# Maxima taken 162 slots ahead, 22 bursts without them, and keys and queries loaded apart for maxima and scores

## The chip, the cores and the metric

The kernel runs on one core of a Trainium2 chip. The metric is device time in microseconds of one execution; before the change it is 1759.31 us, the median of three runs (1758.76 to 1759.72).

## The reference

Two attention layers with 32 heads of 16 over the same input x (2048 rows of 512) are mixed by a gate.

```python
g = _sigmoid((x * gate_w).sum(-1, keepdims=True))
a = _A_ref(x, A_wqkv, A_wo)          # full softmax attention, 2048 x 2048 for each head
b = _B_ref(x, B_wq, B_wk, B_wv, B_wo, B_beta)
return g * a + (1 - g) * b
```

A is ordinary attention: `softmax(q k^T / 4) v`, then an output product. B cuts the sequence into four segments of 512. Inside a segment it is causal softmax attention; to that comes, for the segments after the first, `phi(q) M / (phi(q) z)` from a running memory `M = sum phi(k) v^T`, `z = sum phi(k)` over the earlier segments, mixed by `sigmoid(beta)` for each head. All arithmetic is float32; the kernel writes a factor as a high and a low part in a rounded float32 form and multiplies (high, low), (low, high) and (high, high).

## The kernel before, in words

**Units, slots, bursts.** The work on scores is cut into units `(side, g, c)`: four heads (`g` of 8 groups) and a chunk `c` of 512 queries. An A unit has 64 slots (4 heads x 16 blocks of 128 keys), a B unit 10. They alternate, A0, B0, A1, B1 and so on, 32 of each, 2368 slots in all. In a slot TensorE makes one score product (`score_part`, line 1063: 128 keys x 512 queries into one of three banks `st`), and ScalarE takes its exponential (line 1086, or 1083 for two of B's slots) into a tile `p`. A burst is three slots; behind them TensorE multiplies earlier `p` by the values (`some_values`, line 155, bank `ops`), or makes other products.

**Maxima.** The softmax needs the maximum of each query's scores first. So every score is also made the other way round (`max_product`, line 242: 128 queries x 512 keys, into one of four banks `sm`), and VectorE reduces it (line 275 for A; for B's triangle a masked form, line 290). There are as many maxima parts as slots (list `maxs`). Part `m = n + LEAD` is made in slot `n`, with `LEAD = 96`; the first 96 are made before the first score. When a unit's parts are done, GpSimd joins them (`finish_max`), TensorE transposes them (`transpose_max`), and two small transfers put them, high and low part, into rows 48 and 49 of the unit's tile of queries. The same rows of the tiles of keys hold ones, so that the score product subtracts the maximum.

**Tiles.** A tile of queries or keys is 128 x 2 x 512: two heads in each half of the partitions, at rows 0 and 64. Of each half 48 rows are the high and low parts (queries high, high, low; keys high, low, high), and two are the maxima or ones. Scores and maxima read the same tile: the keys wait in a ring of 8 (A) or 2 (B) from their maxima to their scores, the queries in a ring of 6. A product uses only one half of TensorE's rows, so a score on one half and a maximum on the other stand beside each other: slot `n` has its score on half `n % 2`, its maximum on the other.

**DRAM.** The projections write queries and keys to DRAM as 32 rows (16 high, 16 low; `qd`, `kd`); a tile of A is loaded by four transfers (16 and 32 rows for each half), one of B by six. All run on SyncE's queue, in order. Loads run `PRE = 20` parts ahead of the maxima; the last value product of a burst waits for the loads that the next burst needs (`wait_early`).

**Before the first score** come the projections, in steps of 12 matmuls of 512 columns (`slot()`, line 366), with a hand-written table of what follows in which step. 38 steps are A's, 48 are B's (four chunks of four query, four value and four key tiles); `s0` is B's first. A tile goes from its bank through ScalarE (`full`, then its high part, lines 432 and 433), and VectorE subtracts for the low part (line 440). In 24 of B's steps, from the twelfth on, a group of four maxima follows the products (`some_max`).

**Beside the scores** in the main loop: the output product of the chunk before, and for the first eight A units a projection of later queries. Both are lists of 12 (`shared`), four in a burst, so three bursts behind each A unit's end carry them instead of values; each is two products of 64 rows, one into `ops`, one into an `sm` bank that is lent for the time (`row_halves`). At the end ScalarE copies both banks out and GpSimd adds them (`join_halves`, lines 972 and 973). In the last 90 slots (`wide`) there are no maxima left to make.

Of the kernel before, what the change touches and what calls it, by code (L numbers as in the profile page):

```python
# [21 lines left out]
DH = 16  # L22
CH = 512
# [20 lines left out]
NKA, NKB = 8, 2  # L44
# [3 lines left out]
def gated_mix(ctx, tc, x, xT, wqkv, a_wo, b_wq, b_wk, b_wv, b_wo, beta, gate_w, out):  # L48
# [48 lines left out]
    qp = ctx.enter_context(tc.tile_pool(name="qp", bufs=6))  # L97
# [16 lines left out]

    maxs = []
    for k in range(NU):
        mine = {u: iter(range(32)) for u in range(2)}
        bs = [k - 1] if 0 < k < NU - 1 else [k - 1, k] if k else []  # L120
        theirs = {r: [(unit("B", b), (r, i)) for b in bs for i in range(5)] for r in range(2)}
        start, apart = (33, (3, 3)) if k == 1 else (6, (9, 3)) if k < NU - 1 else (23, (3, 3))
# [13 lines left out]
    assert len(maxs) == nS and all(first[u] + LEAD - last_max[u] > 24 for u in units)  # L136

    qt, kt_ = {}, {}

    def raw(t):  # L140
# [16 lines left out]
    def wait_early(n):  # L157

        loads_ = []
        for m in range(n + 1 + LEAD, n + 1 + BURST + LEAD):  # L160
            if m < nS:
                u, (r, i) = maxs[m]
                loads_ += lands.pop(("q", u, r), []) + lands.pop(("k", u, r, u[2] if u[0] == "B" else i // 8), [])
        for u, j in slots[n + 1:n + 1 + BURST]:
# [6 lines left out]
    def load_rows(t, r, src, hs, side, halves):  # L171

        if side == "B":
            return [nc.sync.dma_start(raw(t)[64 * r + 16 * i:64 * r + 16 * i + 16], src[x, hs].rearrange("h d t -> d h t"))  # L174
                    for i, x in enumerate(halves)]
        at_ = (0, 16, 48) if halves[1] == 0 else (0, 32, 48)
        return [nc.sync.dma_start(raw(t)[64 * r + a:64 * r + b], src[0:b - a, hs]) for a, b in zip(at_, at_[1:])]

    def load_q(u):
        side, g, c = u  # L180
        t = qp.tile([128, 2, CH], F32R, tag="q", name=f"q{side}{g}{c}")
        src = qd[side, g // 2, c]
        for r in range(2):
            hs = slice(4 * (g % 2) + 2 * r, 4 * (g % 2) + 2 * r + 2)
            lands["q", u, r] = load_rows(t, r, src, hs, side, (0, 0, 1))
        qt[u] = t

    def load_k(u, kc):
# [1244 lines left out]
```

## Time and profile before

| | |
|---|---|
| median of three runs | 1759.31 us |
| the profiled execution, its own time | 1757.79 us |
| span of its profile, first to last instruction | 1756.1 us |
| first score on TensorE | 280.08 us |
| busy: TensorE matmul, VectorE, ScalarE, GpSimd | 1747.3, 1600.3, 1449.4, 774.3 us |
| granted TensorE clock | 1.00 throughout |

The profile is of one execution; its times stand from the span's start. Line numbers (L275) are those of the kernel. In rows, `out<-in` are tiles, "PE" is TensorE, "PEld" its weight loads, "DVE" VectorE, "ACT" ScalarE, "POOL" GpSimd, "SP" SyncE. The end of a matmul is modelled, so a full PE line does not say that TensorE is at its peak; for the other engines busy time is what they ran.

### The profile page before, as it was taken

The numbers are of one execution on the slowest core, as the hardware profiler recorded it, in microseconds if no ns is written. First come the engines' busy times: TensorE is split into PE (matmuls) and PEld (weight loads), VectorE is DVE, ScalarE is ACT, GpSimd is POOL, SyncE is SP. The second block draws the span as 40 slices with busy tenths as digits, with TensorE's granted clock in tenths as the row PEclk, the third lists the DMA queues.
The fourth block names the chain that finished last, engine by engine and source line by source line (L and its number), as shares of the span: only waits on it lengthen the run. The fifth ranks groups of instructions, "written<-read, shape, count | busy, mean of one in ns | idle before, by whom it ended". The sixth has DMA issues, their size and how long they took to land.

```text
span 1756.1 us, 43955 instructions
## 1 busy us (share of the span) xinstructions
PE 1747.3 (100%) x16365; PEld 951.2 (54%) x16365; DVE 1600.3 (91%) x3327; ACT 1449.4 (83%) x2793; POOL 774.3 (44%) x1022
## 2 busy tenths in 40 slices
PE   9999999999999999999999999999999999999999
PEld 7887775555454454455444445455545445545454
DVE  7757788999999999999999999999999999999931
ACT  6545557898898988888889888888898889888884
POOL 3543233334453437453535454545344353545452
PEclk9999999999999999999999999999999999999999
DMA  6786567435453435444545454444444443444542
GB/s 209 258 285 222 199 217 218 117 98 139 122 155 110 137 110 165 142 136 135 143 122 151 126 142 129 133 142 124 148 130 146 130 135 111 144 125 133 150 160 62
DMA packets 149396, 261.77 MB, mean 149 GB/s; under 512 B 39064, under 2 KB 61624, under 8 KB 148672
## 3 DMA queue, kind: packets, MB, share of 16 engines
q1 hardware_dynamic: 146640, 254.42, 48.1%
q0 software_dynamic: 2400, 4.29, 0.9%
q8 instruction: 130, 2.13, 0.5%
q14 instruction: 82, 0.67, 0.1%
q10 hardware_dynamic: 144, 0.26, 0.1%
HBM read 174.39 MB, written 83.25 MB: 147 GB/s over the span
## 4 chain that ended last, share of the span: by engine, by line
PE 97%; DMA 1%; POOL 1%; ACT 0%; SPq 0%; DVE 0%; issue 0%; ACTq 0%; DVEq 0%; POOLq 0%
PE ops L155 35%; PE st L1063 27%; PE sm L242 15%; PE pr L366 9%; PE sm L155 4%; PE pair L366 4%; PE mt_ps L232 0%; PE tps L831 0%; PE sm L1063 0%; POOL rcp L1187 0%; SPq L174 0%; DMA vs<-wqkv 0%; ACT p L1086 0%; DMA qA<-qdA 0%; PE mps L845 0%; DMA qB<-mt 0%
## 5 line engine op out<-in xcount | busy, mean ns | idle before, releaser
L1086 ACT ACTIVATE p<-st 128x512 f32<-128x512 f32 x2261 | 1188.4, 605 | 139.9 <-PE sm L242 91.3
L275 DVE TENSOR_REDUCE pm<-sm 128x1 f32<-128x512 f32 x2048 | 1276.1, 681 | 14.6 <-PE sm L242 11.9
L242 PE MATMUL sm<-kA,qA 48*128 48x512 f32 x2048 | 694.7, 433 | 0.1
L1063 PE MATMUL st<-qA,kA 50*128 50x512 f32 x2014 | 665.8, 433 | 0.0
L155 PE MATMUL ops<-p,vA 128*17 128x256 f32 (+3 forms) x7160 | 560.9, 414 | 2.6 <-DMA rec<-odB 2.1
L1063 PEld LDWEIGHTS st<-qA,kA 50*128 50x128 f32 x2014 | 331.2, 185 | 388.6 <-ACT p L1086 349.1
L242 PEld LDWEIGHTS sm<-kA,qA 48*128 48x128 f32 x2048 | 339.2, 185 | 23.7 <-DVE pm L275 8.4
L155 PEld LDWEIGHTS ops<-p,vA 128*17 128x17 f32 x7160 | 149.9, 96 | 227.2 <-issue 186.7
L1187 POOL TENSOR_TENSOR rcp<-rec,minus 128x32 f32<-128x32 f32 x43 | 234.8, 5460 | 59.8 <-DMA rec<-dend 55.4
L290 DVE CUSTOM_DVE_ANT_0 rest<-sm,mask 128x128 f32<-128x128 f32 (+3 forms) x512 | 246.2, 481 | 3.9 <-PE sm L242 3.5
L1067 POOL TENSOR_SCALAR_AFFINE_SELECT p<-p 128x512 f32<-128x512 f32 x128 | 79.5, 637 | 293.4 <-ACT p L1086 283.2
L242 PE MATMUL sm<-kB,qB 48*128 48x128 f32 (+3 forms) x512 | 160.1, 373 | 0.0
L1063 PE MATMUL st<-qB,kB 50*128 50x512 f32 (+1 forms) x495 | 98.6, 319 | 0.3 <-ACT mt L235 0.3
L1063 PEld LDWEIGHTS st<-qB,kB 50*128 50x128 f32 x495 | 72.2, 186 | 47.0 <-ACT p L1086 32.2
L214 POOL TENSOR_TENSOR dm<-pm 128x32 f32<-128x32 f32 x32 | 7.9, 246 | 185.3 <-DVE pm L275 185.3
L155 PE MATMUL ops<-p,vB 128*17 128x128 f32 (+3 forms) x1504 | 87.9, 350 | 0.0
L242 PEld LDWEIGHTS sm<-kB,qB 48*128 48x128 f32 x512 | 84.5, 184 | 0.7
L437 POOL TENSOR_SCALAR mn<-full 128x512 f32<-128x512 f32 x24 | 37.0, 1542 | 75.5 <-ACT full L432 75.5
L223 POOL CAST ms<-pm 128x16 fp32r<-128x16 f32 x32 | 6.3, 196 | 124.0 <-DVE pm L290 124.0
L155 PEld LDWEIGHTS ops<-p,vB 128*17 128x17 f32 x1504 | 33.4, 96 | 28.6 <-issue 27.4
L1203 POOL TENSOR_TENSOR v<-v,inv 128x512 f32<-128x512 f32 x31 | 39.8, 1284 | 20.1 <-DMA inv<-rdA 12.3
L155 PE MATMUL sm<-wA,blk 64*128 64x512 f32 (+1 forms) x144 | 46.7, 405 | 0.0
(325 smaller groups left out, 1905.4 us busy)
## 6 DMA issues: line engine op xcount, KB each, us to landing
kA<-kdA SPq DMA_DIRECT2D x256, 128.0 KB
vA<-vdA SPq DMA_DIRECT2D x31, 544.0 KB
kA<-kdA SPq DMA_DIRECT2D x256, 64.0 KB
qB<-qdB SPq DMA_DIRECT2D x192, 64.0 KB
kB<-kdB SPq DMA_DIRECT2D x192, 64.0 KB
kdA<-q SPq DMA_DIRECT2D x32, 256.0 KB
qdB<-q SPq DMA_DIRECT2D x32, 256.0 KB
qA<-qdA SPq DMA_DIRECT2D x64, 128.0 KB
```

The costliest lines, as they stand in the source:

```text
L155: behind[0] = nc.tensor.matmul(*args, **kw)
L214: nc.gpsimd.tensor_sub(dm, pm[:, :, :, 2:4], pm[:, :, :, 0:2])
L242: nc.tensor.matmul(ps[:, n0:n0 + n], rows(qt[u][:, :, s * 128:(s + 1) * 128], h, 48), rows(k[:, :, k0:k0 + n], h, 48), start=True, stop=True)
L275: nc.vector.tensor_reduce(pm[:, h, s, kc:kc + 1], ps, axis=AX.X, op=ALU.max, negate=True)
L290: nc.vector.tensor_tensor_reduce(out=tri["rest"][:, 0:w], in0=ps[:, n0:n0 + w], in1=tri["mask"][:, CH - w:], scale=-1.0, scalar=3.0e38, op ...
L366: nc.tensor.matmul(ps, l, r, start=start, stop=stop)
L437: nc.gpsimd.tensor_scalar_min(ph["mn"], full, 0.0)
L1063: nc.tensor.matmul(ps[:, n0:n0 + CH - q0], rows(k[:, :, b * 128:(b + 1) * 128], h, 50), rows(q[:, :, q0:], h, 50), start=True, stop=True)
L1067: nc.gpsimd.affine_select(out=x, in_=x, pattern=[[0, 4], [1, 128]], base=0, channel_multiplier=-1, compare_op=ALU.is_ge, fill=0.0)
L1086: nc.scalar.activation(p[:, h], ps, AF.Exp, scale=SCALE)
L1187: eng.tensor_tensor(r, rec, minus, op=ALU.pow)
L1203: eng.tensor_mul(k["v"], k["v"], k["inv"])
```

## The change

- `FIRST = LEAD + len(thin)`, 162 maxima parts, are made before the first score. `some_max` follows each of B's steps 4 to 47 but steps 18, 30 and 42. The first loads are issued at `s0`, `s0 + 1`, `s0 + 2`. B's first maxima now begin with the main loop.
- For each of the first 22 A units one burst is `thin`: it has no maxima. It is the burst behind the unit's last output products, the one in which the two banks are copied out. `due_at[n]` says which part is due in slot `n`; behind the 22nd thin burst the lead is 96 parts as before.
- `half` and `heads_of` choose the head of each slot so that a score stands on the other half than the maximum beside it, since the parity of maxima shifts by three at each thin burst.
- `qd`, `kd` have 48 rows, in the order of the tile, so that a tile is loaded by two transfers of 48 rows; each projection tile is stored by three transfers instead of two (its high part twice for keys and queries alike).
- Tiles are loaded once for maxima (rings of 3 for A keys, 2 for B keys, 2 and 2 for queries) and once more for scores (4 A keys, 1 B keys, 2 A queries, 1 B queries), the latter `AHEAD = 24` slots ahead (`score_loads`). The rows of maxima are sent to the score tile when it is loaded, or when they are transposed, whichever is later. Only the score rings need rows of ones.
- The low parts of B's projection tiles, and those of B's three weights, are subtracted on GpSimd instead of VectorE.
- The closing tiles have buffers of their own choice.

```diff
-NKA, NKB = 8, 2
+NK = 10
+AHEAD = 24
+THIN = 22
...
-                rows_ = [32, 8, CH] if side == "A" else [2, 8, DH, CH]
+                rows_ = [48, 8, CH]
...
+    thin = set()
+    for k in range(THIN):
+        t = -(-(end[unit("A", k)] + 2) // BURST) * BURST + 3 * BURST
+        thin.update(range(t, t + BURST))
+    FIRST = LEAD + len(thin)
+    due_at = [FIRST]
+    for n in range(nS + LEAD):
+        due_at.append(due_at[-1] + (n not in thin))
...
-        bs = [k - 1] if 0 < k < NU - 1 else [k - 1, k] if k else []
+        bs = {0: [], 1: [], 2: [0], 3: [1, 2], NU - 1: [k - 1, k]}.get(k, [k - 1])
...
-    kbuf = {"A": [kp.tile([128, 2, CH], F32R, name=f"kA{i}") for i in range(NKA)],
-            "B": [kp.tile([128, 2, CH], F32R, name=f"kB{i}") for i in range(NKB)]}
-    knext = {"A": 0, "B": 0}
+    kbuf = [kp.tile([128, 2, CH], F32R, name=f"k{i}") for i in range(NK)]
+    qbuf = [kp.tile([128, 2, CH], F32R, name=f"q{i}") for i in range(6)]
+    ring = {("k", "A", 1): kbuf[0:4], ("k", "B", 1): kbuf[4:5], ("k", "A", 0): kbuf[5:8], ("k", "B", 0): kbuf[8:10],
+            ("q", "A", 1): qbuf[0:2], ("q", "A", 0): qbuf[2:4], ("q", "B", 0): qbuf[4:6]}
...
-        for m in range(n + 1 + LEAD, n + 1 + BURST + LEAD):
+        for m in range(due_at[n + 1], due_at[n + 1 + BURST]):
...
+    def load_rows(t, src, g):
+
+        hs = 4 * (g % 2)
+        return [nc.sync.dma_start(raw(t)[64 * r:64 * r + 48], src[:, hs + 2 * r:hs + 2 * r + 2]) for r in range(2)]
...
+    def store_rows(dst, side, keys, low, t):
+
+        for i in ((1,) if low and keys else (2,) if low else (0, 2) if keys else (0, 1)):
+            to = dst[16 * i:16 * i + 16]
+            if side == "A":
+                nc.sync.dma_start(to.rearrange("d h t -> (d h) t"), t)
+            else:
+                nc.sync.dma_start(to.rearrange("d h t -> h d t"), t)
...
+    def score_loads(n):
+
+        if n < nS:
+            u, j = slots[n]
+            if j == 0:
+                load_q(u, 1)
+            if j % 16 == 0:
+                load_k(u, u[2] if u[0] == "B" else j // 16, 1)
...
-                nc.vector.tensor_sub(q2, full, q1.bitcast(F32))
+                (nc.gpsimd if side == "B" else nc.vector).tensor_sub(q2, full, q1.bitcast(F32))
...
-        staged(tiles_w("k", "wk"), b_wk, ((raw_tile, 33, 2), (raw_tile, 35, 0)), [(41 + k, 3) for k in range(KT)], nc.gpsimd)
+        staged(tiles_w("k", "wk"), b_wk, ((raw_tile, 33, 2), (raw_tile, 35, 0)), [(41 + k, 3) for k in range(KT)], nc.gpsimd, eng=P)
...
-        for i, t in enumerate(kbuf["A"] + kbuf["B"]):
+        for i, t in enumerate(kbuf[0:5]):
...
-        for n in range(5):
-            post_at(s0 + 6 + 3 * n, 2, lambda n=n: loads(16 * n))
+        for n in range(3):
+            post_at(s0 + n, 2, lambda n=n: loads(16 * n))
+        for n in range(AHEAD):
+            post_at(s0 + 36 + n // 3, 1, lambda n=n: score_loads(n))
-        for n in range(12, 64):
+        for n in range(4, 48):
             if n in (18, 30, 42):
                 post_at(s0 + n, 3, lambda c=n // 12: mem_q(c))
-            elif n // 12 > 2 or n % 12 < 8:
+            else:
                 post_at(s0 + n, 3, some_max)
...
-        h = (0, 2, 1, 3)[j % 4]
+        h = heads_of[n]
...
+        score_loads(n + AHEAD)
         if n < nS:
             score_part(n)
-        m = n + LEAD
-        if m < nS:
+        m = due_at[n] if n < nS + LEAD else n + LEAD
+        if n not in thin and m < nS:
             loads(m + PRE)
```

More of the change, by code (lines that the diff above doesn't have):

```diff
@@ L113, in gated_mix @@
     nS = len(slots)
+    thin = set()
[6 more added lines that the diff above has]
+        due_at.append(due_at[-1] + (n not in thin))
+    slot_of = {due_at[n]: n for n in range(nS) if n not in thin}
+    n_of = lambda m: slot_of.get(m, m - FIRST)
     maxs = []
@@ L348, in gated_mix @@
             nc.tensor.matmul(idle[:, :128], identf, identf, start=True, stop=True)
-        ones = wk1.tile([2, CH], F32, name="ones")
-        nc.vector.memset(ones, 1.0)
+        one = wk1.tile([128, CH], F32, tag="mn", name="one")
+        nc.vector.memset(one[0:2], 1.0)
+        ones = dr.tile([2, CH], F32, name="ones")
+        nc.gpsimd.dma_start(ones, one[0:2])
         now = [0]
@@ L416, in xchunk, with qk_tile @@
             return xT[:, c * CH:(c + 1) * CH]
-        def qk_tile(w, xc, o, dst, then=None, side="B", bank=None):
+        def qk_tile(w, xc, o, dst, then=None, side="B", bank=None, keys=False):
             ps = bank() if bank else pr_ps.tile([128, CH], F32, tag="pr", name="pr")
@@ L705, in tiles_x2 @@
         def tiles_x2():
-            x2["t"] = [[qp.tile([128, 2, CH], F32R, tag="q", name="x2") for _ in range(2)] for _ in range(2)]
+            x2["t"] = [qbuf[2:4], qbuf[4:6]]
             xs[2] = lambda a, k: x2["t"][a][k // 2][:, k % 2]
@@ L907, in gated_mix @@
             slot()
-        assert not rows_left
+        assert not rows_left and mnext[0] == FIRST
     gp = ctx.enter_context(tc.tile_pool(name="gp", bufs=1, reuse_waits="tile"))
@@ L1046, in gated_mix @@
     queue = []
+    heads_of = {}
+    for u in units:
+        for j0 in range(0, SLOTS[u[0]] - 3, 4):
+            of = {0: [0, 1], 1: [2, 3]}
+            for j in range(j0, j0 + 4):
+                heads_of[first[u] + j] = of[half[first[u] + j]].pop(0)
+        if u[0] == "B":
+            for j in (8, 9):
+                heads_of[first[u] + j] = 2 * half[first[u] + j]
     def score_part(n):
```

136 lines of the change are left out of this document (76 added, 60 removed).

## The prediction

> **What bounds the kernel now.** I read the page first, then the windows (busy time of each engine per stretch), then the time line of single engines inside two stretches: the one in which maxima are left out, and the one that takes them over.
>
> ```profile
> span 1756.1 us, 43955 instructions
> PE 1747.3 (100%) x16365; PEld 951.2 (54%) x16365; DVE 1600.3 (91%) x3327; ACT 1449.4 (83%) x2793; POOL 774.3 (44%) x1022
> ...
> DVE  7757788999999999999999999999999999999931
> ```
>
> TensorE is busy all the time, but its matmul ends are modelled, so this only says that it never waits long. VectorE's line of digits changes at slice 7: before it, in the projections, VectorE has room; behind it, in the main loop, it has none. The windows (columns: PE, PEld, DVE, ACT and POOL busy with their instruction counts, clock, DMA share, GB/s) say it in numbers:
>
> ```profile
> 100.00:125.00 25.00, 25.00 (x112) 20.70 (x111) 16.65 (x25) 13.48 (x24) 13.85 (x21) 1.00 0.94 320
> 121.16:142.93 21.77, 21.77 (x98) 17.98 (x96) 7.73 (x14) 12.12 (x21) 8.39 (x12) 1.00 0.85 288
> 177.03:188.05 11.02, 11.02 (x50) 9.07 (x49) 9.17 (x18) 5.93 (x11) 4.59 (x3) 1.00 0.84 318
> 400.00:500.00 100.00, 100.00 (x1036) 49.44 (x1030) 99.67 (x214) 89.67 (x175) 46.48 (x65) 1.00 0.48 136
> 327.31:331.46 4.15, 4.15 (x40) 1.87 (x36) 4.15 (x12) 4.15 (x9) 3.14 (x4) 1.00 0.00 0
> 740.26:744.39 4.13, 4.13 (x40) 1.86 (x36) 4.13 (x12) 4.13 (x9) 3.21 (x4) 1.00 0.52 142
> 1012.71:1016.85 4.14, 4.14 (x40) 1.86 (x36) 4.14 (x12) 4.14 (x9) 3.21 (x4) 1.00 0.61 153
> ```
>
> The first three lie in the projections, the fourth in the middle of the main loop: VectorE 99.67 of 100 us, ScalarE 89.67. The last three are, for A units 0, 9 and 15, the two bursts behind the unit's last output products (a burst is three score slots and what TensorE does behind them). There ScalarE too is busy without a gap, 4.13 of 4.13 us. That is where the change acts, so I look inside, at A unit 9, whose scores end at slot 730 and whose thin burst is slots 741 to 743. ScalarE, VectorE and TensorE there:
>
> ```profile
> 739.12 1.09 ACT L1083 ACTIVATE p<-st 128x512 f32<-128x512 f32 x2 [0.49 <-PE st L1063]
> 740.09 0.61 ACT L1086 ACTIVATE p<-st 128x512 f32<-128x512 f32 x1
> 740.56 0.61 ACT L972 COPY res<-ops 128x512 f32<-128x512 f32 x1
> 741.03 0.63 ACT L973 COPY bot<-sm 128x512 f32<-128x512 f32 x1
> 741.50 3.11 ACT L1086 ACTIVATE p<-st 128x512 f32<-128x512 f32 x6
> 744.93 0.60 ACT L1086 ACTIVATE p<-st 128x512 f32<-128x512 f32 x1 [0.32 <-PE sm L242]
> 742.27 2.52 DVE L275 TENSOR_REDUCE pm<-sm 128x1 f32<-128x512 f32 x4
> 744.97 1.29 DVE L275 TENSOR_REDUCE pm<-sm 128x1 f32<-128x512 f32 x2 [0.17 <-PE sm L242]
> 740.26 0.45 PE L242 MATMUL sm<-kB,qB 48*128 48x128 f32 x2
> 741.56 0.84 PE L155 MATMUL ops<-p,vB 128*17 128x384 f32 x8
> 742.33 0.50 PE L1063 MATMUL st<-qA,kA 50*128 50x512 f32 x1
> 743.20 0.49 PE L1063 MATMUL st<-qA,kA 50*128 50x512 f32 x1
> 744.39 0.50 PE L1063 MATMUL st<-qA,kA 50*128 50x512 f32 x1
> ```
>
> The burst from 740.26 is the thin one. ScalarE starts 739.12 and then runs eleven operations with no idle time to 744.61: three exponentials, the two copies that join the output products, six exponentials. It has waited for nothing since 739.12. TensorE's third score of the second burst comes at 743.20 because its bank is read by the third of the six exponentials (741.50 + three times about 0.48, and the latency). And VectorE, which is behind by two maxima when the stretch begins, has caught up when it ends: at 744.97 it waits for TensorE. So this stretch is set by ScalarE, and every other one by VectorE or by TensorE's own pace.
>
> **The change, part by part.**
>
> Maxima ahead. 162 maxima instead of 96 are taken before the first score. They are taken in groups of four at the end of a projection step (12 matmuls of 512 columns): 24 groups before; now 41, at every step from the fourth to the 47th of the B part but three. The price of a group, in TensorE's time line:
>
> ```profile
> 276.47 0.73 PE L242 MATMUL sm<-kA,qA 48*128 48x512 f32 x4
> 277.13 0.50 PE L366 MATMUL pr<-wqh,wkl 128*128 128x512 f32 x1
> ...
> 280.08 0.50 PE L1063 MATMUL st<-qA,kA 50*128 50x512 f32 x1
> ```
>
> Group and step together take 280.08 - 276.47 = 3.61 us. Steps without a group: the window 121.16 to 142.93 is eight of them, 2.72 each; 177.03 to 188.05 is four, 2.755 each. The new groups stand in those eight steps, in those four and in four like them of the next chunk: 8 x 0.89 + 8 x 0.855 = 13.9 us; the last group, of two, adds about 0.5. TensorE has no wait in those windows, so all of it is on the path: +14.4 us.
>
> VectorE in those steps. A main-loop maximum costs it 0.598 us (below). Four steps with groups take 14.4 us; VectorE has there 9.17 + 16 x 0.598 of work, less four subtractions that go to GpSimd:
>
> ```profile
> L440 DVE TENSOR_TENSOR q<-full,q x31: 677/684/965, 116.8 to 279.4; 128x512 fp32r<-128x512 f32 x31
> L485 POOL TENSOR_TENSOR q<-full,q x4: 1286/1288/1594, 102.8 to 114.1; 128x512 fp32r<-128x512 f32 x4
> L437 POOL TENSOR_SCALAR mn<-full x24: 1479/1487/2016, 135.7 to 250.1; 128x512 f32<-128x512 f32 x24
> ```
>
> 9.17 + 9.57 - 4 x 0.684 = 16.0 us, 1.6 more than the steps take, twice: at most +3.2, at least 0 if the four banks absorb it. I take +2.5, near the upper end, since the gate sums bunch there too.
>
> Work moved to GpSimd. 32 subtractions (0.684 us on VectorE, 1.29 on GpSimd) and 12 of the weight splits. A k step then costs GpSimd 1.49 + 1.29 = 2.8 us of 3.61: it fits. It is tightest in the first eight steps of the B part, where eight splits, four subtractions and the sends of the rows of ones queue on GpSimd; behind them stand the copies that free `full` and, behind those on ScalarE's queue, the copies that free the banks. Bounds 0 (cover holds) to 3 us (two subtractions late by a split each); I take +0.5.
>
> Loads and stores. Each k and q tile is stored in three transfers instead of two, and loaded twice (once for maxima, once for scores) instead of once:
>
> ```profile
> q1 hardware_dynamic: 146640, 254.42, 48.1%
> kA<-kdA SPq DMA_DIRECT2D x256, 128.0 KB
> kA<-kdA SPq DMA_DIRECT2D x256, 64.0 KB
> kB<-kdB SPq DMA_DIRECT2D x192, 64.0 KB
> ...
> kdA<-q SPq DMA_DIRECT2D x14, 256.0 KB
> qdB<-q SPq DMA_DIRECT2D x8, 256.0 KB
> ```
>
> Loads: (256 x 192 + 192 x 64) KB of keys and a quarter of the first and all of the second again for queries, 88 MB; as much again over 1400 us of main loop is 63 GB/s on the 136 of the window at 400, whose share of 0.48 would go to about 0.7. That hides. The number of issues on SP hardly changes: 32 a unit pair become 28. Loads are issued 20 to 24 slots ahead, over ten microseconds. The new waits on SP (a ring of three or four tiles, one for B scores) each follow a last read that lies 12 slots or more back; behind one would stand the stores and value loads, for which the next burst's last value product, and so the next three scores, would wait. I cost them 0. In the projections the last two rows, from 100 to 125 us, are 5.8 MB of 8.0; half as much again, and 1.6 MB of first loads now at steps 0 to 2 instead of 6 to 18, meet a share of 0.94. The store buffers have three turns, the first maxima four steps (11 us). Bounds 0 to 13 us (4.5 MB at 340 GB/s, all of it waited for); I take +0.5, since TensorE has no wait in that window now, at 0.94.
>
> The rest I cost at nothing: the new order of heads keeps each score beside a maximum of the other row half, as now; a unit's rows of maxima are sent when its score tile of queries is loaded, 24 slots ahead, or when they are transposed if that is later, as now; the second unit's transposition moves from a burst to a projection step, TensorE's time in both; the last 90 slots, whose lead is 96 again, and the closing tiles keep their times. Their cover is the lead in slots; without it, the next burst's scores would wait for one landing.
>
> Thin bursts. 22 bursts lose their three maxima. VectorE's price is in a run of eleven:
>
> ```profile
> 899.91 6.66 DVE L275 TENSOR_REDUCE pm<-sm 128x1 f32<-128x512 f32 x11
> 774.93 0.50 PE L1063 MATMUL st<-qA,kA 50*128 50x512 f32 x1
> 776.62 0.49 PE L1063 MATMUL st<-qA,kA 50*128 50x512 f32 x1
> ```
>
> (6.66 - 0.68) / 10 = 0.598 us; 66 of them are 39.5 us. By the Trainium skill (Perfetto Trace Analysis, "Identifying the Most-Contended Engine"), the engine with the highest occupancy is the one to relieve, TensorE's matmul time being no measure; that is VectorE here, and by this rule the main loop would shorten by the 39.5 us. The rows of the stretch say otherwise: the number of bursts stays, every other burst keeps its three maxima, and the two bursts concerned are set by ScalarE's eleven operations, none of which goes. Without its maxima the thin burst ends sooner, and the next waits for banks that the same exponentials free. What is late next is nothing: VectorE idles about 1.8 us where it now catches up. Bounds: 0, and the two bursts at TensorE's unhindered pace (776.62 - 774.93 = 1.69 each), 4.13 - 3.38 = 0.75 us, 16.5 in all. ScalarE's rows have no gap, so I take 0.1 each: -2 us.
>
> Sum, against the profiled execution (1757.8 us, span 1756.1): 14.4 + 2.5 + 0.5 + 0.5 - 2 = +15.9, 1773.7 us. The runs' median, 1759.3, is 1.5 above that execution: 1775.2.
>
> **Rivals.**
> VectorE pays (faster). The main loop moves at VectorE's pace as a whole and the maxima taken away come off it: 17.9 - 39.5 = -21.6, 1737.7 us. For it: 99.67 of 100. Against: VectorE waits at 744.97, so its backlog does not outlast the stretch. It decides from a gain of 17.9 / 22 = 0.81 us a thin burst.
> TensorE pays. The two bursts fall to 1.69 us each: 17.9 - 16.5 = +1.4, 1760.7 us. Against: the same eleven operations.
> The transfers bound the projections: 1757.8 + 14.4 + 2.5 + 13 + 1.5 = 1789 us. For it: 0.94. Against: stores are not waited for by TensorE.
>
> **How the numbers follow.** Forecast 0.68, with a range of its own from 1768 to 1782; VectorE pays 0.13; TensorE pays 0.08; transfers 0.11. A measurement can tell about 0.2% (3.5 us) from no change. Faster: the first rival and a little of the second, 0.15; same: most of the second, 0.07; slower 0.78. The range, 1755 to 1788, leaves out the first rival and the far end of the last.
>
> **What would show it.** Right: TensorE's first score about 15 to 18 us later than 280.08, steps of 3.61 us at 41 groups, a main loop as long as before to within 3 us, VectorE idle about 1.8 us in each thin stretch while ScalarE stays full there, DMA share near 0.7 with no wait of TensorE on a load. Wrong: thin stretches shorter than 4.1 us, a first score later than 300 us, or gaps on TensorE behind `kA` or `qA` loads.

## The result, and the profile after

The changed kernel takes 1832.11 us (median of four runs, 1828.8 to 1836.17) against 1759.03 us before on the same chip: 1.0417 times as long, 95% interval 1.0388 to 1.0445. The prediction was 1775.2 us, range 1755 to 1788. It had the sign and missed most of the size: 73 us lost where 16 were forecast. The profile below is of the execution that took 1835.41 us, 3.3 above the median, so the parts in it add up to 77.6 us and not to 73.

The page of the changed kernel, in the lines that answer to those of before:

```profile
span 1833.7 us, 43806 instructions
PE 1786.4 (97%) x16365; PEld 964.5 (53%) x16365; DVE 1586.3 (87%) x3283; ACT 1451.5 (79%) x2794; POOL 824.6 (45%) x1057
DVE  6648886799998999899999999999999899999841
q1 hardware_dynamic: 168400, 359.27, 74.8%
```

TensorE, 100% busy before, is at 97%: it now waits. The transfers of SP's queue take 74.8% of the transfer engines' time (48.1% before). The windows say where (columns as in the prediction):

```profile
100.00:125.00 25.00, 24.12 (x106) 19.31 (x105) 12.73 (x17) 9.12 (x16) 13.79 (x16) 1.00 1.03 372
125.00:150.00 25.00, 20.42 (x82) 13.72 (x83) 12.08 (x20) 9.72 (x16) 18.40 (x22) 0.86 0.81 273
300.00:325.00 25.00, 16.82 (x74) 10.97 (x72) 8.94 (x16) 10.53 (x17) 10.95 (x14) 0.88 0.77 228
325.00:350.00 25.00, 18.86 (x161) 9.02 (x163) 18.16 (x51) 13.06 (x25) 7.25 (x11) 0.71 0.78 196
400.00:500.00 100.00, 99.75 (x1024) 49.14 (x1017) 96.42 (x204) 89.68 (x175) 35.69 (x53) 1.00 0.79 192
```

From 100 to 125 us the transfer engines are full (share 1.03, 372 GB/s). Behind that, and again where the main loop starts, TensorE stands still and its granted clock falls to 0.86 and 0.71. In the main loop the transfers' share is 0.79, against 0.48 before and the 0.7 that was foreseen.

The span grew by 77.6 us, in three places. The first score product starts at 316.29 us instead of 280.08: 36.2 us in the projections. The first 24 bursts of the main loop (from the first score to that of the 25th burst) take 14.3 us more, nearly all of it in one stop, from 320.1 to 331.1, and the slow bursts behind it. The rest of the main loop takes 27.1 us more, in stops of 1 to 5 us, most of them at changes of units. The tail is as long as before.

**The stop at the start of the main loop.** The time lines of GpSimd, VectorE and TensorE (start, length, engine, line, what; in brackets the idle time before it and what ended it):

```profile
317.49 1.28 POOL L499 TENSOR_TENSOR q<-full,q 128x512 fp32r<-128x512 f32 x1 [2.39 <-ACT q L492]
318.71 0.58 POOL L1079 DMA_DIRECT2D vA<-vdA  x1
319.29 2.44 POOL L1088 DMA_DIRECT2D gA<-gd  x4
321.65 1.83 POOL L1088 DMA_DIRECT2D gB<-gd  x3
328.66 0.59 POOL L1088 DMA_DIRECT2D gB<-gd  x1 [5.18 <-DMA vA<-vdA]
329.23 0.55 POOL L1093 MEMSET mask<- 128x512 f32 x1
329.86 0.29 POOL L1094 TENSOR_SCALAR_AFFINE_SELECT mask<-mask 128x128 f32<-128x128 f32 x1
330.18 0.29 DVE L348 CUSTOM_DVE_ANT_0 rest<-sm,mask 128x128 f32<-128x128 f32 x1 [12.41 <-POOL mask L1094]
331.14 1.26 PE L300 MATMUL sm<-k,q 48*128 48x512 f32 x2 [11.08 <-DVE pm L333]
338.87 0.79 PE L1136 MATMUL st<-q,k 50*128 50x512 f32 x1
340.98 0.50 PE L1136 MATMUL st<-q,k 50*128 50x512 f32 x1
```

The last moved subtraction (L499) is now the work ahead of the value load, the gate copies and the mask on GpSimd's queue. GpSimd itself stands still for 5.18 us of this, until the value load has landed. The mask is ready at 330.15. B's first masked reduction has waited 12.41 us for it, the four banks stay full meanwhile, and TensorE stops for 11.08 us. Then it runs slower: the first score product of a burst takes 0.79 us until 338.9 and 0.50 from 341.0 on. By the Trainium skill (TensorE: Matmul & The Clock Gate, "Part 1: The HAM clock gate") an idle window of about 3.4 us halves TensorE's clock until it has been busy for about as long. The 0.71 of the window from 325 agrees with the halving: half speed up to 339.6 us would give it. The slow time behind the stop was longer here, some 8 us.

**A thin stretch.** A unit 9 again, the window over its thin burst and the next:

```profile
799.65:803.85 4.20, 4.07 (x38) 1.56 (x35) 2.26 (x5) 4.20 (x9) 3.21 (x4) 1.00 0.42 110
```

and the time line of ScalarE and VectorE there:

```profile
799.48 0.61 ACT L1159 ACTIVATE p<-st 128x512 f32<-128x512 f32 x1
800.04 0.58 ACT L1036 COPY res<-ops 128x512 f32<-128x512 f32 x1
800.52 0.59 ACT L1037 COPY bot<-sm 128x512 f32<-128x512 f32 x1
801.00 3.07 ACT L1159 ACTIVATE p<-st 128x512 f32<-128x512 f32 x6
802.31 1.89 DVE L333 TENSOR_REDUCE pm<-sm 128x1 f32<-128x512 f32 x3 [1.94 <-PE sm L300]
```

4.20 us, 4.13 before. ScalarE is full, 4.20 of 4.20; VectorE idles 1.94 us. This is what was forecast (1.8 us of idle time, next to no gain).

**A late load.** The window over the loads of a change of units, late in the main loop:

```profile
1700.00:1710.00 10.00, 10.00 (x122) 4.69 (x120) 10.00 (x18) 8.96 (x19) 2.35 (x6) 1.00 1.06 247
```

the chain of work that ended last, there (start, length, what):

```profile
1696.92 6.53 DMA k<-kdB
1703.47 9.24 DMA q<-qdA
1712.77 2.66 DMA k<-kdA
```

and where it ends, in TensorE's time line:

```profile
1715.40 0.58 PE L193 MATMUL ops<-p,vA 128*17 128x128 f32 x2 [5.18 <-DMA k<-kdA]
```

Loads for scores and for maxima of both sides, values and output rows come together here. The transfer engines are full (1.06, where the same work before, from 1630 to 1640 us, has 0.52), one load takes 9.24 us, the next in the chain is issued only when it has landed, and TensorE waits 5.18 us.

### The profile page after: what moved, and what is told of

Read it like the earlier page. It is cut to its first block, busy times and chain, and to the rows that moved or that the text cites. A ratio compares the mean times of both kernels' runs of the same rounds, so it can differ in the third digit from the quotient of the medians.

```text
span 1833.7 us, 43806 instructions
## 1 busy us (share of the span) xinstructions
PE 1786.4 (97%) x16365; PEld 964.5 (53%) x16365; DVE 1586.3 (87%) x3283; ACT 1451.5 (79%) x2794; POOL 824.6 (45%) x1057
## 3 DMA queue, kind: packets, MB, share of 16 engines
q1 hardware_dynamic: 168400, 359.27, 74.8%
## 4 chain that ended last, share of the span: by engine, by line
PE 76%; DMA 11%; DVE 5%; ACT 4%; POOL 2%; issue 1%; SPq 1%; ACTq 0%; DVEq 0%; POOLq 0%
PE ops L193 30%; PE st L1136 23%; PE sm L300 12%; PE pr L426 5%; PE sm L193 3%; DVE pm L333 2%; DMA k<-kdB 2%; DMA q<-qdA 1%; DMA k<-kdA 1%; DMA raw<-xT 1%; PE pair L426 1%; ACT p L1159 1%; POOL rcp L1260 1%; SPq L213 1%; DMA vdA<-vs 1%
## 5 line engine op out<-in xcount | busy, mean ns | idle before, releaser
L300 PE MATMUL sm<-k,q 48*128 48x512 f32 (+3 forms) x2560 | 805.7, 425 | 16.3 <-DVE pm L333 12.8
L1136 PE MATMUL st<-q,k 50*128 50x512 f32 (+1 forms) x2021 | 674.3, 436 | 1.0
L1136 PEld LDWEIGHTS st<-q,k 50*128 50x128 f32 x2021 | 332.9, 186 | 396.3 <-ACT p L1159 355.7
L300 PEld LDWEIGHTS sm<-k,q 48*128 48x128 f32 x2560 | 385.2, 186 | 45.2 <-DVE pm L333 24.1
L1136 PE MATMUL st<-qsB,k 50*128 50x512 f32 (+1 forms) x488 | 99.2, 322 | 0.3 <-ACT mt L293 0.3
L1136 PEld LDWEIGHTS st<-qsB,k 50*128 50x128 f32 x488 | 72.4, 188 | 48.4 <-ACT p L1159 33.7
L1276 POOL TENSOR_TENSOR vM<-vM,inv 128x512 f32<-128x512 f32 x12 | 15.4, 1283 | 93.7 <-DMA inv<-rdM 78.4
L503 ACT ACTIVATE ex<-mn 128x512 f32<-128x512 f32 x24 | 15.2, 632 | 45.1 <-DVE ph L508 29.7
L499 POOL TENSOR_TENSOR q<-full,q 128x512 fp32r<-128x512 f32 x32 | 42.5, 1327 | 15.4 <-ACT q L492 7.7
```

Of the source, the lines that this page charges most:

```text
L300: nc.tensor.matmul(ps[:, n0:n0 + n], rows(qm[u][:, :, s * 128:(s + 1) * 128], h, 48), rows(k[:, :, k0:k0 + n], h, 48), start=True, stop=True)
L499: (nc.gpsimd if side == "B" else nc.vector).tensor_sub(q2, full, q1.bitcast(F32))
L1136: nc.tensor.matmul(ps[:, n0:n0 + CH - q0], rows(k[:, :, b * 128:(b + 1) * 128], h, 50), rows(q[:, :, q0:], h, 50), start=True, stop=True)
```

## The experiments

The kernels are variants of the changed one, except the last. "First score" and "loop" (first to last score product) are from TensorE's time line of one profile each; "start" is what the first 24 bursts take more than before. The medians of the variants are of four or five executions. Five of the profiles have the same code, or nearly, up to the first score (after, e1, e6, e7, e8), and it comes between 310.4 and 316.3 us in them: a difference of less than 6 us in that column says nothing by itself.

| kernel | median us | ratio to before, 95% | first score | loop | start |
|---|---|---|---|---|---|
| before | 1759.0 | 1 | 280.1 | 1452.4 | 0 |
| after | 1832.1 | 1.0388 to 1.0445 | 316.3 | 1493.9 | 14.3 |
| e1 mask first | 1825.6 | 1.0364 to 1.0395 | 310.4 | 1487.5 | 11.0 |
| e2 subtractions on VectorE | 1828.6 | 1.0377 to 1.0412 | 312.2 | 1491.5 | 12.1 |
| e3 rows of 32 | 1862.4 | 1.0572 to 1.0603 | 301.0 | 1538.8 | 15.0 |
| e4 maxima 16 rows | 4803.1 | 2.7266 to 2.7348 | | | |
| e5 no thin bursts | 1851.3 | 1.0504 to 1.0539 | 311.8 | 1515.6 | 12.7 |
| e6 thin in the middle | 1836.8 | 1.0397 to 1.0468 | 316.0 | 1499.3 | 16.2 |
| e7 16 rows and zeros | 1817.3 | 1.0316 to 1.0346 | 313.1 | 1477.8 | 15.2 |
| e8 score loads on GpSimd | 1907.0 | 1.0825 to 1.0874 | 314.9 | 1574.9 | 13.0 |
| e9 = e1 + e2 + e3 | 1867.7 | 1.0581 to 1.0659 | 309.0 | 1533.2 | 11.3 |
| e10 all light | 1801.6 | 1.0225 to 1.0259 | 307.9 | 1467.5 | 2.2 |
| e11 all light, no thin | 1781.0 | 1.0106 to 1.0136 | 290.0 | 1465.9 | 0.0 |
| e12 before + 8 groups | 1767.8 | 1.0035 to 1.0063 | 288.6 | 1453.9 | 0.0 |

**e1, the mask first.**

```diff
+    tri["mask"] = ...; nc.gpsimd.memset(...); nc.gpsimd.affine_select(...)
     load_v(units[0], nc.gpsimd)
     for (s, c), t in gate.items():
         nc.gpsimd.dma_start(t, ...)
-    tri["mask"] = ...; nc.gpsimd.memset(...); nc.gpsimd.affine_select(...)
```

> Only the order of GpSimd's queue is changed: the mask of the B maxima is made ahead of the value load and the eight gate copies. Theory 1 (the main loop's first stall of 12.4 us is the first masked reduction waiting for a mask that stands on GpSimd's queue behind a gate copy's wait): that wait falls to under 2 us, the first unit gives back 11 to 14 us with the lowered clock that follows it, the first score stays at 316 us, and the time goes from 1832 to 1818-1822 us (1.034 to 1.036 of before). Rival (the same transfers that hold the gate copies back hold the first loads too): another wait takes its place and the time stays within 4 us of 1832.

The wait for the mask went from 12.41 to 1.86 us. But TensorE stops again, from 315.6 to 323.5; the time lines of e1:

```profile
313.71 0.29 DVE L348 CUSTOM_DVE_ANT_0 rest<-sm,mask 128x128 f32<-128x128 f32 x1 [1.86 <-POOL mask L1089]
313.89 0.58 POOL L1079 DMA_DIRECT2D vA<-vdA  x1 [0.21 <-issue]
323.47 1.48 PE L193 MATMUL ops<-p,vA 128*17 128x384 f32 x8 [7.84 <-DMA vA<-vdA]
```

The value load, too, stood behind the last subtraction, and it needs 9.6 us while SP's queue still sends twelve stores of `kdB` (302.52 to 318.96). Of the 14.3 us at the start only 3.3 went. The rival is right in kind: taking away one late thing showed the next, and that one is a transfer. Its number failed narrowly, since the median came 6.5 us below the changed kernel's and not within 4; most of the difference lies in the first score, inside the scatter.

**e2, subtractions and weight splits of the B part back on VectorE.**

```diff
-                (nc.gpsimd if side == "B" else nc.vector).tensor_sub(q2, full, q1.bitcast(F32))
+                nc.vector.tensor_sub(q2, full, q1.bitcast(F32))
...
-        staged(tiles_w("q", "xb"), b_wq, ..., nc.gpsimd, eng=P)      (and "v", "k")
+        staged(tiles_w("q", "xb"), b_wq, ..., nc.gpsimd)
```

> The subtractions of the B tiles and the splits of the three B weights go back to VectorE; all else as after the change. Theory 1 (the stalls of 21.8 us in the projections beyond the groups' own 14.4 are GpSimd being late): first score from 316 to 296-304 us, and since GpSimd's queue is then short the mask is early as well: 12 us less in the first unit, in all about 1800-1808 us. Rival 2 (the stalls are the transfers, three stores a tile and doubled loads): first score 312 or later; VectorE gets 22 us of subtractions and 8 us of splits back into steps that it already fills, which may add up to 6 us; only the mask's 12 us go, 1818-1824 us.

The first score comes at 312.2, inside the scatter, where theory 1 had 296 to 304: GpSimd being late was not what the projections paid. Two rows of the waits of e2 from 100 to 320 us (who waits for what: us in total, times, longest):

```profile
ACT q L492 <- DMA qdB<-q: 9.5, 2, 6.4
PE sm L300 <- DMA k<-kdA: 5.6, 1, 5.6
```

and its window over the k steps of the second chunk:

```profile
200.00:225.00 25.00, 24.90 (x172) 17.46 (x171) 24.93 (x47) 11.11 (x21) 11.04 (x14) 1.00 0.65 217
```

ScalarE waits 9.5 us for stores of queries to release the store buffers, the first maxima wait 5.6 us for their keys, and with the subtractions back VectorE is full, 24.93 of 25. With GpSimd's queue short the mask is ready at 312.7, just behind the first score, and yet the start loses 12.1 us. The waits are now for stores of `kdB`: ScalarE's last copy waits 3.10 us for one, VectorE's last subtraction 4.49 us, with the masked reductions behind it, and the slow clock follows. So the 12 us that both theories gave to the mask did not come back, and 1828.6 us lies above rival 2's range too.

**e3, rows of 32: two stores a tile, four transfers to load one.**

```diff
-                rows_ = [48, 8, CH]
+                rows_ = [32, 8, CH]
...
-        return [nc.sync.dma_start(raw(t)[64 * r:64 * r + 48], src[:, hs + 2 * r:hs + 2 * r + 2]) for r in range(2)]
+        at_ = (0, 32, 48) if keys else (0, 16, 48)
+        return [nc.sync.dma_start(raw(t)[64 * r + a:64 * r + b], src[0:b - a, hs + 2 * r:hs + 2 * r + 2])
+                for r in range(2) for a, b in zip(at_, at_[1:])]
...
-        for i in ((1,) if low and keys else (2,) if low else (0, 2) if keys else (0, 1)):
+        for i in (low,):
```

> Keys and queries are kept as 32 rows as before the change (two stores a tile instead of three) and each tile is loaded by four transfers (16 and 32 rows) instead of two; maxima and scores still load apart. Rival 2 (transfers bound the projections): a third of the store bytes goes, 4 of 12 MB in the projections, first score from 316 to 300-308 us. Theory 1 (GpSimd): first score within 3 us of 316. For the main loop: if its 27 us of scattered losses come from the bytes loaded twice, it stays within 5 us of 1494 us from first to last score; if from the shape of the 48-row transfers (mean packet of 4 KB 274 ns against 222 before), it loses 10 us or more.

The first score comes at 301.0, 15 us sooner than after the change and 9 sooner than the earliest of its kind, as rival 2 had it. The edit changes the stores and the loads, but other runs tell them apart. The first group of maxima starts at 124.0 to 125.3 us in the three runs with two stores (e3, e9, e10) and at 129.0 to 132.6 in the seven with three and the same lead (after, e1, e2, e4, e6, e7 and e8), also in e4 and e7, whose loads for maxima carry a third of the bytes. So the third store, where the transfer engines are full, costs some 4 to 8 us by then; of the rest of the 15 us the split is not shown. The loop loses 45 us more. The bytes loaded are the same and the packets have 4 KB in both, so neither expectation on the loop's side fits. What has doubled is the count of loads: by its time line SP's queue spends 1063 of 1500 us of e3's loop issuing transfers, 664 of 1470 after the change. In the waits of e3's loop TensorE stands behind the rows of maxima, which SP sends behind twice as many loads:

```profile
PE ops L193 <- DMA qsB<-mt: 22.4, 6, 5.5
```

**e4 and e7, loads for maxima with a third of the bytes.** The maxima are taken from the high halves. In e4 the products run over 16 rows; in e7 over 48 again, 32 of them zeros.

```diff
-        return [nc.sync.dma_start(raw(t)[64 * r:64 * r + 48], src[:, ...]) for r in range(2)]
+        return [nc.sync.dma_start(raw(t)[64 * r:64 * r + n], src[:n, ...]) for r in range(2)]    # n = 48 if scores else 16
...
-        nc.tensor.matmul(ps[:, n0:n0 + n], rows(qm[u]..., h, 48), rows(k..., h, 48), ...)
+        nc.tensor.matmul(ps[:, n0:n0 + n], rows(qm[u]..., h, 16), rows(k..., h, 16), ...)        # e4 only
+        nc.gpsimd.dma_start(raw(t)[64 * r + 16:64 * r + 48], zeros...)                           # e7 only, once, qbuf[2:6]
```

> The maxima are taken from the high halves alone (16 rows of 48; the maximum need only be near), so that the loads for maxima carry a third of the bytes; the count of transfers, matmuls and reductions is as after the change. Theory 3 (the main loop's scattered losses of 27 us are loads that land late because all bytes are loaded twice): 59 of the 88 MB that were added go, the share of the DMA engines goes from 0.79 to about 0.6 in the main loop, which loses 15 to 27 us; in the projections up to 8 us. Rival (they are late because of the queue of issues, not of the bytes): main loop within 5 us of 1494. In both cases the 14.4 us of the groups and the mask's 12 us stay.

> As the run with 16 rows, but the products of the maxima go over 48 rows again, of which rows 16 to 47 of the queries are zeros set once (the maximum is that of the high halves). The loads for maxima carry a third of the bytes. First, on the clock of 0.54 in that run: if it fell because the products used 16 rows, the clock is back at 0.98 or more; if because of the data, it stays low. With the clock back, theory 3 (the main loop's scattered losses are the bytes loaded twice): DMA share about 0.6 instead of 0.75, main loop 1494 to 1470-1480 us. Rival (the queue of issues on SP): main loop within 5 us of 1494.

e4 took 4803 us and says nothing on loads. TensorE's time line in the middle of its loop:

```profile
1003.22 0.79 PE L1136 MATMUL st<-q,k 50*128 50x512 f32 x1
1003.95 0.79 PE L300 MATMUL sm<-k,q 16*128 16x512 f32 x1
```

the same in the kernel after the change, in A unit 9, and where its clock is low too (0.83 from 1710 to 1720 us):

```profile
801.74 0.50 PE L1136 MATMUL st<-q,k 50*128 50x512 f32 x1
801.74 0.50 PE L300 MATMUL sm<-k,q 48*128 48x512 f32 x1
...
1715.92 0.79 PE L1136 MATMUL st<-q,k 50*128 50x512 f32 x1
1715.92 0.79 PE L300 MATMUL sm<-k,q 48*128 48x512 f32 x1
```

and a window of e4:

```profile
1000.00:1100.00 100.00, 99.75 (x318) 39.63 (x317) 34.38 (x68) 33.31 (x58) 10.68 (x18) 0.50 0.22 58
```

A score and a maximum, which start together after the change (in the two row halves), here start 0.72 us apart, one after the other, and the clock stays at 0.50. It is not the low clock that parts them, since at 1715.92 the pair starts together. With zeros in e7 the clock is back (0.988 over the run): it is the count of rows in the product, not the data and not the bytes loaded. e7 then tells the bytes. In its loop the transfers' share is 0.60 (0.78 after the change),

```profile
330.00:1780.00 1450.00, 1441.01 (x14412) 719.30 (x14408) 1352.48 (x2906) 1285.80 (x2495) 650.09 (x866) 1.00 0.60 156
```

and behind its start it loses 10.2 us (25.4 - 15.2) instead of 27.1; the loop, 1477.8 us, lies in the range of theory 3. So about six tenths of the scattered losses go with the bytes loaded twice.

**e5, no thin bursts.** Lead, groups and the order of the maxima are as before the change.

```diff
-THIN = 22
+THIN = 0
...
-        for n in range(4, 48):
+        for n in range(12, 64):
...
-            else:
+            elif n // 12 > 2 or n % 12 < 8:
                 post_at(s0 + n, 3, some_max)
```

> The change without its thin bursts: the lead is 96 slots again, 24 groups in the projections at the steps of the kernel before, every burst keeps its maxima; 48 rows, three stores, loads apart and GpSimd's subtractions stay. Theory T (the predicted price of the groups is right and a thin burst is worth nothing): the first score comes 14 to 17 us sooner, at 296-302 us; the main loop, first to last score, stays at 1494 us within 4 apart from its first unit; 1812-1820 us. Rival V (a thin burst saves VectorE's 1.8 us): the main loop becomes 39 us longer, 1855 us. If the early start of the groups is also what makes the transfers late, the first score comes below 290 us.

1851 us looked like rival V, but it isn't. Burst by burst, the thin one and its next together are no shorter in the changed kernel than with their maxima in e5: 0.0 to 0.4 us longer in 20 of the 22 units, 1.4 in the other two, both near a stop. The 22 us that the loop adds lie in stops for loads and rows of maxima, up to 5.5 us each. Theory T's numbers failed as well: the loop was to stay, and the first score hardly moves, though TensorE had some 14 us less to do. The transfers take it back, at the first group of maxima (TensorE's time line of e5):

```profile
187.01 1.41 PE L300 MATMUL sm<-k,q 48*128 48x512 f32 x4 [13.84 <-DMA k<-kdA]
```

Why the loop has more stops for loads without the thin bursts, at the same bytes, stays open; between e10 and e11, with fewer bytes, no such difference of the loops is left.

**e6, the thin bursts in the middle of the unit.**

```diff
-        t = -(-(end[unit("A", k)] + 2) // BURST) * BURST + 3 * BURST
+        t = -(-(end[unit("A", k)] + 2) // BURST) * BURST + 12 * BURST
```

> The 22 thin bursts are moved nine bursts later, from the second burst behind the join of a unit's output to the middle of the next A unit; nothing else. Theory P (maxima left out pay only where VectorE is the one that is behind; behind the join it is ScalarE, in the middle VectorE runs at 1.79 us a burst against 1.69 of TensorE): each thin burst takes 1.69 us or less and gives back what VectorE is behind by then, up to four banks: 22 x 1.0 to 1.8 = 22 to 40 us, 1792-1810 us. Rival (the pace of the middle is TensorE's or ScalarE's as well): within 4 us of 1832.

No gain that the medians show: 1836.8 us, and the intervals of the two overlap. Theory P's 22 to 40 us are out; the rival's 4 us are missed by less than 1. A thin burst is shorter by about 0.2 us than the same burst with its maxima (here 1.86 instead of 2.03 before the change), no burst around it is shorter, and some 5 us in all are less than the stops for loads scatter. ScalarE and VectorE of e6 around the thin burst from 869.27 to 871.13:

```profile
868.09 3.29 ACT L1159 ACTIVATE p<-st 128x512 f32<-128x512 f32 x6 [0.18 <-PE sm L300]
871.66 1.58 ACT L1159 ACTIVATE p<-st 128x512 f32<-128x512 f32 x3 [0.28 <-PE sm L300]
869.81 0.69 DVE L333 TENSOR_REDUCE pm<-sm 128x1 f32<-128x512 f32 x1
871.71 0.42 DVE L348 CUSTOM_DVE_ANT_0 rest<-sm,mask 128x256 f32<-128x256 f32 x1 [1.21 <-PE sm L300]
```

VectorE idles 1.21 us and little is gained by it: three exponentials take ScalarE 1.64 us, and TensorE's bursts go on at 1.67 and 1.92 us in turn. The pace of 1.69 us that the prediction took for TensorE unhindered is thus that of every second burst. VectorE's 99.67 of 100 us before the change was an engine that just kept up.

**e8, the loads for scores on GpSimd's queue** in the main loop.

```diff
+        queue = nc.gpsimd if scores and main[0] else nc.sync
-        return [nc.sync.dma_start(...
+        return [queue.dma_start(...
```

> In the main loop the loads for scores (keys and queries) are issued by GpSimd's queue instead of SP's; bytes and shapes as after the change. If the scattered losses of the main loop are loads that stand behind others on SP's queue, they shrink: main loop 1494 to 1475-1485 us. If it is the bytes, or the transfers themselves that are long under load, no change within 5 us, or worse by what GpSimd's own late work (octets, maxima rows) holds back: up to 1510 us.

81 us more in the loop, worse than any expectation. In e8's groups GpSimd spends 134.8 us on issuing loads of keys alone (0.54 us each):

```profile
L216 POOL DMA_DIRECT2D k<-kdA x252 | 134.8, 537 | 17.5 <-PE sm L303 7.9 <-issue 3.3 <-DMA k<-kdA 2.5
```

and in the chain of work that ended last GpSimd has 10% (2% after the change), in part for the factors of the output rows that it makes late. The run does not tell SP's order from the bytes: it put the loads behind another queue's work.

**e9, e1 to e3 together**, the edits as above.

> Three of the single edits together: rows of 32 (two stores a tile, four transfers to load one), the mask ahead of the value load, the subtractions and weight splits of the B part back on VectorE. For the projections: the groups alone (14.4 us) would give a first score at 294.5 us; with 32 rows alone it came at 301.0. If GpSimd's subtractions are the remaining 6.5 us: 294-297 us. If they are not, 300-302 us. For the first unit: with mask and value load both early and fewer transfers pending, its loss falls from 15 us to under 5 us; if it stays above 9 us, it is the transfers or the clock. The rest of the main loop keeps the losses of the run with 32 rows (84 us beyond the first unit): 1835-1850 us in all.

The first score, 309.0, is 8 us later than in e3 and outside both ranges. VectorE is nearly full with the subtractions (24.40 of its 25 us from 200 to 225), but that stretch is only some 0.4 us longer than in e3. The loss is at the first groups, 5.4 us by the third: VectorE's subtraction at 128.74 waits 7.77 us for a store of queries, and the group's reductions stand behind it. About 3 us more go between 278 and 294. In this pair of runs the subtractions on GpSimd were therefore the better choice for the projections; the order of the mask differs too. The stop for mask and values is gone, but another follows: TensorE waits 6.42 us, until 356.5, for the rows of maxima, which SP sends behind a raw weight load of 7.09 us. The start loses 11.3 us, the branch that names transfers or the clock. The total lies above its range. The 84 us carried over from e3 are 71 in e3's trace (86.4 in the loop, 15.0 of them at the start).

**e10 and e11, everything light**, with and without thin bursts: rows of 32, maxima over 16 rows and zeros, the mask first, subtractions on VectorE; e11 has e5's edit as well.

> All remedies at once, the lead of 162 and the 22 thin bursts kept: rows of 32, maxima from 16 rows (zeros in the other 32 of the queries), the mask early, subtractions and splits on VectorE. If the change's own price is what the prediction took (41 groups for 14.4 us, thin bursts for nothing) and all the rest of the 73 us is transfers and the order on GpSimd's queue: first score 294-298 us, main loop 1452 to 1462 us, 1773-1785 us in all. If the groups themselves cost more (VectorE in the k steps, banks), the first score stays at 300 us or later.

> As the run with all remedies, but without thin bursts: lead 96, 24 groups, maxima in every burst. With the transfers out of the way, the difference of the two is the price of 66 maxima ahead of the first score against 22 thin bursts. By the prediction's terms: first score 14 to 17 us sooner (280-283 us), main loop within 3 us of the other's, 1759-1768 us. By rival V (thin bursts save VectorE's time) the main loop is 39 us longer; by rival P (TensorE's) 16 us longer.

The time lines of e10:

```profile
128.83 0.69 DVE L504 TENSOR_TENSOR q<-full,q 128x512 fp32r<-128x512 f32 x1 [7.51 <-DMA qdB<-q]
307.86 0.40 PE L1147 MATMUL st<-q,k 50*128 50x512 f32 x1
```

and of e11:

```profile
166.20 1.31 PE L302 MATMUL sm<-k,q 48*128 48x512 f32 x4 [6.17 <-DMA k<-kdA]
290.00 0.50 PE L1147 MATMUL st<-q,k 50*128 50x512 f32 x1
```

The last row of each is the first score: between the two the lead of 162 costs 17.9 us, close to the groups' terms (14.4 + 2.5), though each is one profile. The medians differ by 20.6 us. The loops are 1467.5 and 1465.9 us: 22 thin bursts give nothing, also where transfers disturb less. Rivals V and P, 39 and 16 us, are excluded. The thin burst and its next are again 0.0 to 0.5 us longer together in e10, in all 22 units. The start is nearly without loss in both. The other ranges were missed, e10's loop by 5 us, the totals by 17 and 13 us, and the first scores by 10 and 7 us, both for a transfer at the first groups: in e10 VectorE's subtraction waits 7.51 us for a store of queries, with the group's reductions behind it; in e11 the first group waits 6.17 us for its keys, and the clock falls behind it (0.80 from 150 to 175). So even with two stores the transfers at 100 to 165 us are on the path.

**e12, the kernel before with eight groups more.**

```diff
             elif n // 12 > 2 or n % 12 < 8:
                 post_at(s0 + n, 3, some_max)
+            elif n > 12:
+                post_at(s0 + n, 3, again)      # the last four products and reductions once more, into a spare tile
```

> The kernel before the change, with eight groups of four maxima more in the projections: in the k steps of the second and third chunk (20 to 23 and 32 to 35), which have none, the four last maxima are taken once more, product and reduction, into a tile that nobody reads. No load, store or subtraction is added. It measures the group's price by itself, where transfers play no part. By the prediction: 8 x 0.855 = 6.8 us of TensorE and 0 to 3.2 us for VectorE, 1766-1769 us (1.0039 to 1.0057 of before). If the groups in the k steps are what took the rest of the projections (VectorE, the banks, the transpositions beside them), 10 us or more, from 1769 us.

The first score comes 8.6 us later, the median is 8.6 us higher: 1.07 us a group, of which 0.855 are TensorE's by the prediction's rows; the rest, 1.8 us in all, lies within its 0 to 3.2 us for VectorE, and the median of 1767.8 us in the range of 1766 to 1769. No version here beats the kernel before.

## Why the prediction was wrong, step by step

**Maxima ahead, +14.4, and VectorE, +2.5: right.** e12 measures 8.6 us for eight groups, e11 to e10 17.9 us for the whole lead. A step with a group takes 3.61 us where nothing is waited for.

**Thin bursts, -2: right but for the sign of a small term, and for the reason given.** The thin stretch is not shorter than before, about 0.2 us longer in the mean where 0.1 less were forecast, ScalarE full, VectorE idle 1.94 us. Rival V is excluded by e10 against e11, and e6 shows that another place gives about 0.2 us a burst. The rule of the most-contended engine (Trainium skill, Perfetto Trace Analysis, "Identifying the Most-Contended Engine"), by which 39.5 us were to be had from VectorE, does not hold here. In the thin stretch ScalarE was as full, and elsewhere TensorE's bursts went on at their pace without the reductions.

**Work moved to GpSimd, +0.5 (0 to 3): a path missed.** The prediction looked at what stands behind the splits in the middle of the projections and not at what stands behind the last subtraction: the value load, eight gate copies and the mask, for which the first maxima of B wait. In the changed kernel that is the wait that ends last, 12.41 us. But it is not what the move costs by itself: with the mask first (e1) the start loses 11.0 us instead of 14.3, with the subtractions back on VectorE (e2) 12.1, with both and two stores (e9) 11.3, each time with waits for transfers. Lighter loads for maxima alone (e7) leave 15.2, and only all of these together brought it to 2.2 (e10). How the 14.3 us divide stays open.

**Loads and stores, +0.5 (0 to 13): the step that failed, and the largest miss.** Two readings of it were wrong. The first is "stores are not waited for by TensorE". The prediction named the three turns of the store buffers and took them for enough. With the transfer engines at 1.03, ScalarE's copy waits for a store to release its buffer, and the copies that free the banks stand behind it. From the waits of the changed kernel, 100 to 320 us:

```profile
ACT q L492 <- DMA qdB<-q: 7.2, 2, 3.9
```

Before the change, ScalarE's copies waited for no store there. The chain of work that ended last goes through transfers there too: a load of keys of 7.01 us ahead of the first group (from 124.02), one of 6.92 us behind the stores of `kdB` (from 294.28), and a store of 5.83 us that ScalarE's next copy waits for (from 301.26). With two stores instead of three (e3) the first score comes 15 us sooner. That is the rival "the transfers bound the projections", which had 0.11 and a price of 13 us; what is left beyond the groups is some 19. The second reading is "that hides". It took a share of about 0.7, a mean over 100 us, for room at every moment. The mean came out at 0.79, and at the change of units that is shown the share is 1.06 for ten microseconds, a load takes 9 us, and SP's waits, costed at 0, hold back the next: 27.1 us in stops over the loop, of which about six tenths go with the bytes (e7).

**The sum.** 36.2 in the projections (about 17 groups with VectorE, about 19 left for transfers) + 14.3 at the start + 27.1 in the rest of the loop = 77.6 us of the span. The forecast of 15.9 held the first 17, and nearly nothing of the other 60. The 19 are a difference and not measured by themselves: the third store has some 4 to 8 of them by the first group, and how the others divide between stores and doubled first loads is open.

## What to carry to other kernels

When a change moves work to another engine's queue, read that queue to its end, past the last moved instruction: what waits there may be the first thing that the next stage needs. A mean share of the transfer engines hides bunches; price doubled traffic in the window where transfers come together, and ask which buffers its stores hold. An engine that is busy all the time is not the bound until leaving its work out shortens something; here 66 reductions left the loop and it was no shorter (1467.5 us against 1465.9).

## What was not expected of the hardware

In e4 a product over 16 rows did not run beside one over 50, as one over 48 does: starts 0.72 us apart instead of 0.00, with TensorE busy 99.75 of 100 us and yet at a clock of 0.50 for the main loop. The clock fell in e4 with the stop at the start, as in the others, and did not come back; whether the few rows or the gaps between the products keep it there was not tried. And 48 rows loaded in one transfer went better than 16 and 32 in two, although the transfer engines' share was lower with the two (0.69 against 0.78 over the loop): SP's time to issue them had grown from 664 to 1063 us.
